# Loads of values, keys and queries planned one a step, and weight decoding kept out of the first and last round of an attention kernel

## The chip, the cores and the metric

One core of a Trainium2 chip runs the whole program. The metric is the device time of one execution in microseconds (us); lower is better. Kernels are compared by the median of several executions.

## The reference, cut to what matters

Four batches of attention over 12 heads, with a 12x12 mixing of the heads before and after the softmax, feed a two-layer network of 1792 tokens, 768 to 2048 to 768, with an ELU between the layers.

```python
scores = scale * q @ k.T                              # (4, 12, 448, 448), head_dim 64
scores = einsum('bhij,hg->bgij', scores, w_pre)
attn = exp(scores - max) / (sum + 1e-9)
attn = einsum('bhij,hg->bgij', attn, w_post)
x = (attn @ v) laid out as (1792, 768)
h = x @ moe_w_in;  g = where(h > 0, h, exp(min(h, 0)) - 1);  out = g @ moe_w_out
```

The two weight matrices arrive as 8-byte floats; the kernel makes 4-byte floats of them itself ("decoding").

## The kernel before, in words

**Attention.** `attention` (L127) works in 92 steps of one Python loop (L407, variable `j`), 23 for each batch; 23 steps are called a round here (`ROUND`, L376). A batch has four blocks of query rows, which take 5, 6, 6 and 6 steps, so that block 0 starts in step 0 of its round, block 1 in 5, block 2 in 11 and block 3 in 17. What one step does, in the order of the code: `norm` (L268) makes scaled copies `wz` of the post-mixing weights on GpSimd (POOL); `scores` (L249) mixes the raw scores of step j + 2 on TensorE (PE), from which VectorE (DVE) takes the maximum and ScalarE (ACT) the exponential; `send` (L234) starts the DMAs of raw scores computed in the step before; `av` (L299) multiplies by the values of an earlier block; `qk` (L207) computes four heads of raw scores of a later block and `keep_qk` copies them to SBUF; `post` (L280) mixes the heads of step j; then comes planned work (`work`, filled by `plan`, L371), most of it loads and splits of inputs.

**Raw scores.** The raw scores leave `qk` with a head in each tile, and `scores` wants the heads across partitions, so each head of each block is moved from SBUF to SBUF by a DMA on SyncE's queue (`raw<-st`, L242 and L245). A block's twelve heads are computed in three lots, at steps -10, -8, -6 (block 0), -4, -2, -1 (block 1), 1, 3, 5 (block 2) and 7, 9, 11 (block 3) of its round (`RAW_AT`, L377), and sent a step later each. `scores` of the block's first step is issued two steps ahead of that step: in steps -2, 3, 9 and 15 of the round. The last lot of block 2 is thus sent in step 6 and wanted in step 9. The first round differs: the last lot of its block 2 is computed in step 6 and sent in step 7.

**Inputs.** Values (`load_v`, six tiles a batch), keys (`load_k`, six) and queries (`load_q`, one tile a block) are loaded by DMAs that POOL issues (L203, L179, L191). Keys and queries are then split into a high and a low part on DVE and POOL (L185, L186, L197, L198), at fixed steps that the change leaves alone. `av` uses the values of a new batch from step 6 of its round on. A tile pool sets how early a load can go: there are eight buffers for values, four for keys, two for queries.

**Decoding.** `Weights.run` (L66) is a generator: each call of `step` advances it by one piece. A tile of weights takes four pieces: DVE operations L80, L85, L91 and L94, an ACT square L89 with the second, a load of 512 KB (L63) with the first and a store of 256 KB of the tile before (L103) with the second, both DMAs issued by POOL. There are 48 tiles, 24 of each matrix, in all 194 pieces and a last store. In the attention it is called at L436, in every even step from 8 on and in steps 21 and 61, 44 times. In the ELU stage it is called in `elu` (L609), and in the first matrix product after that eight pieces at a time (L684).

**Network.** From step 82 on the `Moe` class starts to load activations and decoded weights. Batches 0 and 1 go through `up` (L590) and `elu` (L601), then L692; batches 2 and 3 through seven products of half size on either side (L984 and L1046). Decoded tiles are read back from DRAM through SyncE's queue (`load_w`, L486), two blocks of hidden units ahead of their use (a block of 128 hidden units is 36 matmuls of `up`), and split into a high part on ACT (L513) and a low part on POOL or DVE (L514).

## Time and profile before

| | |
|---|---|
| three executions | 808.5, 812.62 and 818.0 us; median 812.62 |
| profiled execution | 811.77 us |
| its span, first to last instruction | 810.0 us |
| lies around the span | 1.77 us |
| mean granted clock of TensorE | 0.991 of full speed |
| PE busy in the span | 776.1 us (96%) |

A time of a row counts from the start of the span. The attention runs from about 18 to 356 us, and one round takes 84 us: the scores that are issued in step 9 of the second, third and fourth round start at 148.07, 231.78 and 315.43. The ELU stage of batches 0 and 1 runs to about 483, their second product to 600, and the seven products on either side fill the rest.

### The profile page before, as it was taken

What the parts mean: (1) busy time and instruction counts of PE and PEld (TensorE: products, weight loads), DVE (VectorE), ACT (ScalarE), POOL (GpSimd) and SP (SyncE); (2) the same over time, 40 slices, a digit from 0 to 9 for tenths busy, and PEclk for the clock granted to TensorE, in tenths of its full rate; (3) what the DMA queues carried; (4) which work ended last, traced back from release to release, by engine and by line L of the source; (5) the groups of instructions that cost most, each with busy time, mean ns of one, the idle gap of its engine ahead of it and who ended that gap; (6) DMA issues with size and microseconds to landing.
All of it is one profiled execution on the core that took longest, in us unless ns stands there. A gap on an engine that the chain in (4) does not pass through costs nothing.

```text
span 810.0 us, 25153 instructions
## 1 busy us (share of the span) xinstructions
PE 776.1 (96%) x10014; PEld 631.9 (78%) x10014; DVE 580.3 (72%) x1082; ACT 509.2 (63%) x1092; POOL 408.7 (50%) x529
## 2 busy tenths in 40 slices
PE   7787999899989999899999999999999999999998
PEld 3355676567656666678999999999999989899997
DVE  5685777686768676675988888776357777688962
ACT  3575878687867877785877783223157566665440
POOL 6574645464538353245787773275148877600000
PEclk9899999999999999999999999999999999999999
DMA  6568668756877685846998779987536866653331
GB/s 197 184 205 257 190 207 258 235 190 204 236 222 230 187 240 196 229 135 221 316 308 300 245 234 355 301 308 280 166 125 204 260 206 234 184 160 117 116 123 58
DMA packets 92845, 174.60 MB, mean 216 GB/s; under 512 B 21888, under 2 KB 59556, under 8 KB 92728
## 3 DMA queue, kind: packets, MB, share of 16 engines
q1 hardware_dynamic: 75288, 113.46, 43.7%
q0 software_dynamic: 16896, 58.61, 22.7%
q8 instruction: 79, 1.29, 0.6%
q10 hardware_dynamic: 544, 0.92, 0.3%
q14 instruction: 38, 0.31, 0.1%
HBM read 94.04 MB, written 39.35 MB: 165 GB/s over the span
## 4 chain that ended last, share of the span: by engine, by line
PE 79%; DMA 10%; POOL 3%; issue 3%; DVE 2%; ACT 2%; SPq 1%; POOLq 0%; ACTq 0%
PE h L597 15%; PE y L692 14%; PE y L1046 13%; PE mixed L287 9%; PE s L256 8%; PE xo L308 8%; PE qk L220 7%; PE h L984 6%; DMA raw<-st 4%; DMA sum<-mix 2%; DMA mix<-s 1%; POOL lo L841 1%; ACT p L263 1%; DMA wa<-in 1%; DVE nm L261 1%
## 5 line engine op out<-in xcount | busy, mean ns | idle before, releaser
L263 ACT ACTIVATE p<-s,nm 128x448 f32<-128x448 f32 x180 | 112.9, 634 | 54.2 <-DVE nm L261 53.6
L261 DVE TENSOR_REDUCE nm<-s 128x1 f32<-128x448 f32 x180 | 103.7, 617 | 56.9 <-PE s L256 56.5
L276 POOL TENSOR_SCALAR wz<-wb,rz 128x60 f32<-128x60 f32 x180 | 82.3, 469 | 107.8 <-DVE rz L272 48.0
L287 PEld LDWEIGHTS mixed<-wz,p 64*64 64x64 f32 x5040 | 85.9, 136 | 36.3 <-issue 25.8
L294 ACT COPY at<-mixed 128x480 f32<-128x480 f32 (+1 forms) x184 | 93.3, 566 | 32.1 <-PE mixed L287 30.5
L256 PE MATMUL s<-raw,wa 64*64 64x448 f32 x720 | 93.3, 553 | 16.8 <-DMA raw<-st 9.0
L287 PE MATMUL mixed<-wz,p 64*64 64x60 f32 x5040 | 100.1, 223 | 7.9 <-issue 5.6
L308 PEld LDWEIGHTS xo<-at,v 128*64 128x64 f32 x1536 | 75.8, 135 | 33.1 <-ACT st L230 24.0
L1046 PE MATMUL y<-part,hi 128*128 128x448 f32 x336 | 96.4, 367 | 0.0
L308 PE MATMUL xo<-at,v 128*64 128x120 f32 (+2 forms) x1536 | 86.8, 263 | 0.8 <-DMA v<-in 0.6
L513 ACT CAST hi<-lo 128x1024 fp32r<-128x1024 f32 (+1 forms) x49 | 48.0, 979 | 40.5 <-PE y L1046 34.6
L984 PE MATMUL h<-op,hi 128*128 128x448 f32 x264 | 72.2, 367 | 0.0
L597 PE MATMUL h<-xh,hi 128*128 128x448 f32 x192 | 70.7, 368 | 0.0
L597 PE MATMUL h<-xh,lo 128*128 128x448 f32 x192 | 70.1, 365 | 0.0
L597 PE MATMUL h<-xl,hi 128*128 128x448 f32 x192 | 70.1, 365 | 0.0
L692 PE MATMUL y<-gl,hi 128*128 128x448 f32 x192 | 69.8, 363 | 0.0
L692 PE MATMUL y<-gh,hi 128*128 128x448 f32 x192 | 69.8, 363 | 0.0
L692 PE MATMUL y<-gh,lo 128*128 128x448 f32 x192 | 69.7, 363 | 0.0
L514 DVE TENSOR_TENSOR lo<-lo,hi 128x1024 fp32r<-128x1024 f32 x30 | 37.9, 1263 | 42.2 <-ACT hi L513 40.1
L984 PE MATMUL h<-op,lo 128*128 128x448 f32 x240 | 67.4, 367 | 0.6 <-POOL lo L841 0.6
L1046 PEld LDWEIGHTS y<-part,hi 128*128 128x128 f32 x336 | 63.0, 188 | 6.3
L1046 PE MATMUL y<-part,lo 128*128 128x448 f32 x168 | 61.8, 368 | 0.0
(122 smaller groups left out, 1654.4 us busy)
## 6 DMA issues: line engine op xcount, KB each, us to landing
raw<-st SPq DMA_DIRECT2D x129, 210.0 KB
w<-in POOLq DMA_DIRECT2D x48, 512.0 KB, 6.0
lo<-s SPq DMA_DIRECT2D x58, 256.0 KB
s<-c POOLq DMA_DIRECT2D x48, 256.0 KB, 5.4
v<-in POOLq DMA_DIRECT2D x24, 256.0 KB, 6.6
lo<-half SPq DMA_DIRECT2D x16, 384.0 KB
lo<-sum SPq DMA_DIRECT2D x12, 512.0 KB
raw<-st SPq DMA_DIRECT2D x33, 175.0 KB
```

The lines of the kernel that those rows point to most:

```text
L220: nc.tensor.matmul(got[hh][:m, :S], q[part, hp, :m], k[part], start=i == 0, stop=i == 2)
L256: nc.tensor.matmul(ps[a][w * 64:(w + 1) * 64, :S], wa[half], raws[n % 2][half, ts[0] + w, :], start=True, stop=True)
L261: nc.vector.tensor_reduce(nm, ps[i][:, :S], op=ALU.max, axis=AX.X, negate=True)
L263: nc.scalar.activation(p, ps[i][:, :S], AF.Exp, bias=nm, scale=1.0, accum_out=z[:, i:i + 1])
L276: nc.gpsimd.tensor_scalar_mul(wz, wb, rz[:, i:i + 1])
L287: nc.tensor.matmul(mixed[w][half, i, c, :], p[part, j * 64:(j + 1) * 64], wz[part], start=True, stop=True)
L294: nc.scalar.copy(ats[n][:, :, ts[0]:ts[0] + len(ts), w, :], mixed[w][:, :len(ts)].rearrange("p t c n -> p c t n"))
L308: nc.tensor.matmul(ps[hh * 64:(hh + 1) * 64, w * m:(w + 1) * m].rearrange("p (t r) -> p t r", r=HR), vs[blocks[n][0], hp][:, c, hh * 64:(h ...
L597: self.nc.tensor.matmul(h, w[:, ks], x[:, k, :], start=n == 0, stop=n == 3 * NC - 1)
L692: nc.tensor.matmul(y[u], w[:, ks], g[f][:, u, :], start=f == 0 and n == 0, stop=f == NF - 1 and n == 2)
L984: nc.tensor.matmul(y, p[:, ks], x[:, z], start=q < 2 and k == 0 and n == 0, stop=k == KH - 1 and n == 2, skip_group_check=True)
L1046: nc.tensor.matmul(y, w[:, ks], g[:, x], start=begun is None and k == 0 and n == 0, stop=k == FH - 1 and n == 2, skip_group_check=True)
```

## The change

The loads of values, keys and queries get new steps, at most one load of them a step in each of the later rounds. Decoding starts in step 20 instead of 8, and ends with step 68, the last even one below `3 * ROUND`; the extra calls in steps 21 and 61 go. 25 pieces are decoded beside the attention instead of 44. The ELU stage takes 100 pieces instead of 88, and the product after it 69 or 70 instead of 62 or 63.

```diff
-LATE = 8
+LATE = 20
...
+    Q_AHEAD, V_AT = (7, 6, 6, 7), (19, 21, 24, 25, 26, 27)
...
-            plan(max(at[0] - 5, 1 - LOOK), lambda n=n: load_q(n, nc.gpsimd))
+            plan(max(at[0] - (Q_AHEAD[i] if b else 5), 1 - LOOK), lambda n=n: load_q(n, nc.gpsimd))
...
-                    plan(at[hp // 2] - 5, lambda b=b, hp=hp: load_k(b, hp, nc.gpsimd))
+                    plan(at[hp // 2] - 6 + hp % 2, lambda b=b, hp=hp: load_k(b, hp, nc.gpsimd))
...
-            if i == NB - 1 and b + 1 < B:
-                for w in range(2):
-                    plan(j + w, lambda b=b + 1, hp=2 * u + w: load_v(b, hp))
     for hp in range(NP):
         plan(hp + 2, lambda hp=hp: load_v(0, hp))
+        for b in range(1, B):
+            plan((b - 1) * ROUND + V_AT[hp], lambda b=b, hp=hp: load_v(b, hp))
...
-        if LATE <= j < N and (j % 2 == 0 or j % 40 == 21):
+        if LATE <= j < 3 * ROUND and j % 2 == 0:
             dec.step()
...
-        self.dec.step(2 + (u or f % 2))
+        self.dec.step(3 + (u and f % 4 == 0))
```

In steps of a round the loads move so: values of the next batch from 23, 24, 25, 26, 27, 28 (the last five are steps 1 to 5 of the round that uses them, the first its step 0) to 19, 21, 24, 25, 26, 27; keys of the next batch from 8, 8, 10, 10, 12, 12 to 7, 8, 9, 10, 11, 12; queries from 8, 14, 19, 25 to 6, 13, 18, 23. The first batch's values stay in steps 2 to 7.

On POOL's queue, around the end of the first round and the start of the second, the rows with a DMA or a split of queries stand as follows before (steps 24 to 28; `v` are values, `w` weights to decode, `s` the store of a decoded tile, `q` queries, `wz` the scaled weights that `post` waits for).

```order
L203 DMA v<-in 128x512
L276 TENSOR_SCALAR wz<-wb,rz 128x60 x2
L191 DMA q_2437<-in 128x720
L203 DMA v<-in 128x512
L276 TENSOR_SCALAR wz<-wb,rz 128x60 x2
L63 DMA w<-in 128x1024
L203 DMA v<-in 128x512
L276 TENSOR_SCALAR wz<-wb,rz 128x60 x2
L203 DMA v<-in 128x512
L276 TENSOR_SCALAR wz<-wb,rz 128x60 x2
L103 DMA s_1_74<-c 128x512
L198 TENSOR_TENSOR ql<-q_2437,qh 128x720
```

And now, in steps 22 to 27 (the two values loads of steps 19 and 21 stand ahead of it).

```order
L63 DMA w<-in 128x1024
L198 TENSOR_TENSOR ql<-q_1875,qh 128x720
L276 TENSOR_SCALAR wz<-wb,rz 128x60 x2
L191 DMA q_2268<-in 128x720
L276 TENSOR_SCALAR wz<-wb,rz 128x60 x2
L63 DMA w<-in 128x1024
L203 DMA v<-in 128x512
L276 TENSOR_SCALAR wz<-wb,rz 128x60 x2
L203 DMA v<-in 128x512
L276 TENSOR_SCALAR wz<-wb,rz 128x60 x2
L203 DMA v<-in 128x512
L276 TENSOR_SCALAR wz<-wb,rz 128x60 x2
```

The weights' load of step 26 and the store of step 28 have left this place, weights' loads stand in steps 22 and 24 instead, and the last value is issued a step earlier.

The second place is POOL's queue in steps 10 to 12 of the first round (`k` are keys of the second batch, `kl` their low part). Before:

```order
L63 DMA w<-in 128x1024
L179 DMA k_1230<-in 128x448
L179 DMA k_1232<-in 128x448
L276 TENSOR_SCALAR wz<-wb,rz 128x60 x2
L198 TENSOR_TENSOR ql<-q_1071,qh 128x720
L186 TENSOR_TENSOR kl<-k_1073,kh 128x448
L276 TENSOR_SCALAR wz<-wb,rz 128x60 x2
L63 DMA w<-in 128x1024
L186 TENSOR_TENSOR kl<-k_1075,kh 128x448
L179 DMA k_1404<-in 128x448
L179 DMA k_1406<-in 128x448
L276 TENSOR_SCALAR wz<-wb,rz 128x60 x2
```

Now:

```order
L179 DMA k_1228<-in 128x448
L276 TENSOR_SCALAR wz<-wb,rz 128x60 x2
L198 TENSOR_TENSOR ql<-q_910,qh 128x720
L186 TENSOR_TENSOR kl<-k_995,kh 128x448
L179 DMA k_1315<-in 128x448
L276 TENSOR_SCALAR wz<-wb,rz 128x60 x2
L186 TENSOR_TENSOR kl<-k_1073,kh 128x448
L179 DMA k_1397<-in 128x448
L276 TENSOR_SCALAR wz<-wb,rz 128x60 x2
```

One key's load now stands between the first low part and the `wz` behind it, one fewer behind the second low part, and the weights' loads are gone from here.

## Rows read from the trace of the kernel before

**Rows 1.** Busy time by stretch: length, PE, PEld, DVE, ACT, POOL, PEclk, DMA share, GB/s.
```profile
108.00:192.00 84.00, 80.58 (x1973) 55.52 (x1968) 61.57 (x149) 64.30 (x164) 45.33 (x78) 1.00 0.72 226
384.00:483.00 99.00, 99.00 (x490) 91.77 (x489) 84.47 (x134) 77.52 (x141) 76.10 (x79) 1.00 0.84 278
483.00:600.00 117.00, 117.00 (x584) 109.26 (x583) 78.49 (x106) 40.46 (x66) 46.70 (x64) 1.00 0.75 256
```
**Rows 2.** Timeline of PE, L256: start, duration, what, in brackets idle before and releaser.
```profile
63.43 0.98 PE L256 MATMUL s<-raw,wa 64*64 64x448 f32 x8 [2.75 <-DMA raw<-st]
...
125.63 0.98 PE L256 MATMUL s<-raw,wa 64*64 64x448 f32 x8 [0.27 <-DMA raw<-st]
...
148.07 0.98 PE L256 MATMUL s<-raw,wa 64*64 64x448 f32 x8 [2.35 <-DMA raw<-st]
...
231.78 1.77 PE L256 MATMUL s<-raw,wa 64*64 64x448 f32 x8 [2.09 <-DMA raw<-st]
...
315.43 0.98 PE L256 MATMUL s<-raw,wa 64*64 64x448 f32 x8 [1.50 <-DMA raw<-st]
```
**Rows 3.** Waits of the whole run: total, times, longest.
```profile
PE mixed L287 <- issue: 5.6, 7, 1.7
```
**Rows 4.** Timeline of PE, L287: the first and the last long one of these seven.
```profile
79.75 0.27 PE L287 MATMUL mixed<-wz,p 64*64 64x60 f32 x2 [1.48 <-issue]
...
342.14 0.51 PE L287 MATMUL mixed<-wz,p 64*64 64x60 f32 x19 [1.70 <-issue]
```
**Rows 5.** Busy time by stretch, columns of rows 1: the raw transfers of three rounds.
```profile
104.00:115.00 11.00, 11.00 (x240) 7.96 (x240) 7.25 (x19) 8.61 (x22) 3.27 (x7) 1.00 0.66 205
115.00:126.00 11.00, 10.73 (x296) 7.64 (x289) 8.51 (x22) 8.40 (x23) 6.95 (x13) 1.00 0.76 232
126.00:137.00 11.00, 11.00 (x274) 7.40 (x268) 8.42 (x21) 8.21 (x22) 4.58 (x10) 1.00 0.91 269
...
210.00:221.00 11.00, 11.00 (x274) 7.63 (x272) 8.40 (x21) 9.23 (x25) 5.34 (x10) 1.00 0.90 256
...
294.00:305.00 11.00, 10.47 (x262) 7.27 (x264) 8.29 (x21) 7.65 (x21) 4.12 (x9) 1.00 0.90 272
305.00:316.00 11.00, 9.50 (x260) 6.82 (x256) 6.45 (x17) 9.34 (x24) 5.31 (x10) 1.00 0.65 216
```
**Rows 6.** Timeline of POOL, 126 to 137 us: its DMA issues, start and duration.
```profile
126.26 0.58 POOL L63 DMA_DIRECT2D w<-in  x1
126.85 0.56 POOL L203 DMA_DIRECT2D v<-in  x1
...
130.47 0.59 POOL L203 DMA_DIRECT2D v<-in  x1
...
133.32 0.60 POOL L103 DMA_DIRECT2D s<-c  x1
```
**Rows 7.** DMA issues of the whole run: KB each, median us from issue to landing.
```profile
w<-in POOLq DMA_DIRECT2D x48, 512.0 KB, 6.0
...
s<-c POOLq DMA_DIRECT2D x48, 256.0 KB, 5.4
v<-in POOLq DMA_DIRECT2D x24, 256.0 KB, 6.6
...
q<-in POOLq DMA_DIRECT2D x14, 360.0 KB, 5.4
...
k<-in POOLq DMA_DIRECT2D x18, 224.0 KB, 5.9
```
**Rows 8.** Busy time by stretch, columns of rows 1: right after two of the waits.
```profile
63.00:68.00 5.00, 4.57 (x68) 3.13 (x72) 2.64 (x6) 2.29 (x6) 0.00 (x0) 0.66 0.77 274
...
232.00:237.00 5.00, 5.00 (x84) 2.72 (x80) 2.64 (x6) 2.51 (x7) 0.19 (x1) 0.70 0.63 190
```
**Rows 9.** Groups of instructions in 380 to 480 us: busy, mean ns of one, idle before.
```profile
L514 POOL TENSOR_TENSOR lo<-lo,hi 128x768 fp32r<-128x768 f32 (+1 forms) x14 | 26.5, 1892 | 0.0
...
L85 DVE SCALAR_TENSOR_TENSOR room<-w,room 128x512 int32<-128x512 int32 x20 | 13.9, 694 | 0.4
```

## The prediction

> **What bounds the kernel now.** I read the busy time by stretch first. In the ELU stage and the product behind it PE is busy all of 99.00 and 117.00 us [rows 1]; loads and decoding lie beside it, and what they cost there is nothing as long as it stays so. The attention is different: in a whole round of 84 us PE is busy 80.58, so 3.4 us of idle time are to be had, and DMA runs at a share of 0.72 on average [rows 1]. That is where this change can pay.
>
> Next, PE's timeline in the attention, for what ended each idle stretch. Two kinds stand out. The first is the wait of `scores` for the raw scores' transfers. It is there in five places [rows 2]: at the block 2 of all four rounds (2.75, 2.35, 2.09 and 1.50 us) and, short, at block 1 of the second round (0.27), 8.96 us together. The second kind falls into `post`, with no releaser that the profile shows ("issue"): 5.6 us in seven pieces [rows 3], from 79.75 to 342.14 [rows 4]. I take these for instructions of PE that arrive late, which is an inference: nothing in a row names it.
>
> Why always block 2? The busy time in stretches of 11 us shows it [rows 5]. The DMA share is 0.66, 0.76, 0.91 and it is 0.90 in the two later rounds in just the stretch (126 to 137, 210 to 221, 294 to 305) in which block 2's raw scores travel and behind which PE waits. POOL's timeline shows with what: between 126.26 and 133.32 it issues a load of weights, two of values and a store [rows 6], 512 + 256 + 256 + 256 KB [rows 7]. In the same stretch of 11 us 269 GB/s move, 2.96 MB [rows 5], so these four are 1.31 MB or 44% of it. One stretch earlier the share is 0.76, two earlier 0.66: there is room there.
>
> A wait costs more than its idle time. Behind the first and the fourth of the five the granted clock of the next 5 us is 0.66 and 0.70 on average [rows 8], which mixes the two levels; 5 x 0.34 = 1.7 us and 5 x 0.30 = 1.5 us of PE time went there.
>
> **The change part by part.** The sum is made against the profiled execution, 811.77 us, which lies 0.85 below the median of the runs, 812.62.
>
> Block 2, second round (2.35 us). The weights' load of step 26 and the store of step 28 leave the stretch, the values of steps 27 and 28 come a step earlier, one query is issued near its end. Of 1.31 MB some 0.5 stay, so about 0.8 MB of 2.96 go: 269 GB/s become about 197, less than the 205 at which no wait stands [rows 5]. I take -2.35; bounds 0 and -2.35.
>
> Block 2, fourth round (1.50). No decoding is left there and no query follows: the same 0.8 MB go, and the share 0.90 with them. -1.50; bounds 0 and -1.50.
>
> Block 2, third round (2.09, and 1.5 of clock). Here decoding stays: a load of weights moves from step 50 to 48, a store from 52 to 50, and a query (360 KB) comes in step 52. Of the traffic of the stretch 210 to 221 only about 0.25 MB goes, 256 GB/s become about 233, and that is the rate of the stretch with the 0.76, between no wait and a full one [rows 5]. I take half of both: -1.05 and -0.75; bounds 0 and -3.6.
>
> Block 2, first round (2.75). Its values stay in steps 2 to 7, and a query and a first key now come in steps 6 and 7, before the wait instead of after it: 360 + 224 KB [rows 7] at 263 to 274 GB/s are at most 2.2 us. Against that, the weights' loads of steps 8 and 10 go, but these were issued too late to hold it up. I take +0.5; bounds 0 and +2.2. Its clock loss stays.
>
> Block 1, second round (0.27). Here traffic is added: values in step 21, weights in 22 and 24, against a store in 21 and values in 23 before, some 0.75 MB more, over two stretches that now run at 205 and 232 GB/s [rows 5]. Spread over 22 us that is 34 GB/s, so they come to 239 and 266, just short of the 269 at which PE waits. At that rate 0.75 MB are 2.8 us. I take +1.0, nearer the stretch of 232; bounds -0.27 and +2.8. In the third and fourth rounds it is 0.1 to 0.36 MB: +0.3 each, bounds 0 and +1.3.
>
> The "issue" gaps (5.6). The one at 79.75 stands beside two weights' loads that go, the last at 342.14 beside decoding that goes too. If lateness comes with a full DMA, these have less of it now; if it comes with the place in the program, they only move. I take -2.0; bounds -5.6 and +3, as many again as half of those now seen.
>
> POOL's queue. A key's load (about 0.56 us on POOL, as in rows 6) now stands between the first `kl` and the `wz` behind it, so this `wz` is later by that in each of three rounds; PE asks for it one step on. POOL is busy 45.33 of 84 us [rows 1], and that is the cover: 0, and +1.7 if it is gone. The moved loads wait for no buffer: a value's buffer is free since step 23 or 25 of the round, and a key's since the split just ahead on the same queue. SP's queue has the same instructions in the same order.
>
> ELU stage. 12 more pieces at about 0.69 us [rows 9] are 8.3 us of DVE, which go from 84.47 to 92.8 of 99 [rows 1], 94%. PE fills up to six banks ahead of DVE, so a late DVE alone costs nothing at first. But the handing over gets tight. Counting pieces in the code, the read-back for hidden block 6 now follows the store that it needs by 2 pieces, for block 8 by 3, where it was 18 and 17. A hidden block is 36 matmuls, at 99.00 us for 490 [rows 1] 7.3 us, and a read-back is issued two blocks ahead of its use, 14.5 us. The store needs about 5.4 us to land, the read-back at most the 6.0 of a load of 512 KB [rows 7], the split 1.9 on POOL [rows 9] behind a shorter copy on ACT: some 14 us. It fits, narrowly. 0; bounds 0 and +8.3, if DVE sets the pace. In the product behind it 7 pieces are 4.8 us on a DVE that is busy 78.49 of 117: 0.
>
> Sum: -2.35 - 1.50 - 1.80 + 0.5 + 1.0 + 0.6 - 2.0 = -5.6, so 806.2 us.
>
> There is a rule that speaks against the first three terms. The rows show that DMA share alone does not tell whether raw scores are late: from 305 to 316, where PE waits 1.50, it is only 0.65 [rows 5]. The Trainium skill, "DMA: Bandwidth & Descriptors", section "Why a DMA increments its semaphore by 16 and not by 1", says that a DMA issued on SyncE uses the largest number of engines up to 16 that divides the slowest dimension on both sides; a raw score's transfer ends in 10 partitions, so by it on 10 of the 16. A mean share of 0.65 could then be those ten full, and a load over all 16 puts only 10/16 of its bytes in their way. By that rule the first three terms shrink to 10/16, from 5.65 to 3.5, and the sum would be 808.3. No row here splits the engines.
>
> **The rivals.** *All waits go* but that of the first round: 6.2 us of raw scores, 1.5 of clock and 5.6 of "issue", 13.3 us: 798.5. For it: the emptier first and last rounds, and every moved load goes toward a stretch of lower share. Against: the third round keeps its decoding.
>
> *The raw scores are slow by themselves.* Their own queue is the bound, and what shares the engines with it matters little: 305 to 316 has a share of 0.65 and yet the wait stands behind it. Then block 2 waits as before and only part of the gaps move: 811. Against: blocks 0, 1 and 3 send as many bytes with the same three steps to spare and wait next to nothing.
>
> *The waits move to block 1 and grow* (slower). Place: steps 3 of the second, third and fourth rounds, in which block 1 is wanted; the values of steps 19 and 21 and the weights of 20 to 24 lie ahead of it. Price: in the second round 1.0 MB at 269 GB/s, 3.7 us, in the others 0.5 MB, 1.9 each, and 1.7 of clock behind each: 12.6; with block 2 not relieved, 824.4. It decides as soon as the stretches of 0.66 and 0.76 go past 0.90. For it: block 1 already waits 0.27 in the second round. Against: what is added there is 34 GB/s.
>
> *Decoded weights come late in the ELU stage*: DVE at 94% falls behind, the narrow 14 of 14.5 us is overrun, and PE waits with DVE as the bound: 8.3 us on top of the forecast, 814.5. Against: the six banks, and in the trace of before no idle time of PE in 99 us.
>
> **How the numbers follow.** The forecast has 0.42, all waits gone 0.23, slow raw scores 0.16, late weights 0.10, waits at block 1 0.09. Around the forecast the unknown terms make 801 to 811. A measurement of this kernel tells about 1% from no change, 8.1 us: below 804.5 is faster, above 820.7 slower. Faster: all of 0.23 and three tenths of the forecast's 0.42, 0.36. Slower: the 0.09, and 0.01 for the tail of late weights. The rest, 0.54, is the same. The range reaches from 797, a little below all waits gone, to 817, which takes in late weights and leaves out block 1's case.
>
> **What would show it.** Right: the waits for raw scores at block 2 of the second and fourth rounds are gone from PE's timeline, that of the third is halved, the first's stays near 2.75; the share between steps 3 and 6 of a round falls from 0.90 toward 0.7 and rises between 20 and 2. PE stays at 99% and more in the ELU stage with DVE near 94%. Wrong: a wait of 2 us or more at block 1, waits at block 2 with a share below 0.8 around them, or PE idle between 384 and 600.

## The result and the profile after

The changed kernel takes 819.48 us (median of 22 executions, 811.53 to 825.23), the kernel before 813.92 in the same series (22, 806.68 to 822.37). The ratio is 1.0068, with a 95% interval of 1.0044 to 1.0092. A second series of 12 gave 1.0023 [0.9990, 1.0055] (below); weighted by executions the two make 1.0052 ("pooled" below), about 4 us slower. The forecast was 806.2 us, 5.6 under the execution that it started from, in a range of 797 to 817: its sign was wrong, and the time lies above the range.

The profiled execution of the changed kernel has a span of 817.3 us at a mean granted clock of 0.987, 7.3 us over that of before. First its busy time by stretch, columns of [rows 1]; each round starts a little later than before, so the stretches that answer to [rows 5] are moved by 2 to 6 us.

```profile
106.00:117.00 11.00, 10.95 (x221) 7.64 (x216) 5.96 (x16) 8.17 (x21) 3.77 (x8) 1.00 0.76 227
117.00:128.00 11.00, 10.71 (x298) 7.73 (x296) 8.12 (x22) 8.30 (x23) 6.57 (x12) 1.00 0.92 267
128.00:139.00 11.00, 7.58 (x132) 4.84 (x136) 4.56 (x10) 5.68 (x14) 2.62 (x6) 0.84 0.63 204
214.00:225.00 11.00, 10.06 (x243) 6.66 (x247) 7.79 (x20) 9.15 (x23) 4.63 (x10) 1.00 0.86 274
225.00:236.00 11.00, 8.84 (x200) 5.72 (x189) 5.01 (x12) 5.75 (x15) 3.97 (x8) 0.84 0.57 178
311.00:322.00 11.00, 10.48 (x279) 7.31 (x273) 6.73 (x19) 8.69 (x23) 4.35 (x8) 1.00 0.35 109
384.00:483.00 99.00, 96.94 (x499) 88.53 (x498) 86.32 (x138) 74.97 (x138) 76.48 (x82) 1.00 0.89 294
```

The share of 0.91 that stood at 126 to 137 [rows 5] now stands one stretch earlier (0.92), and behind it PE is busy only 7.58 of 11 us at a granted clock of 0.84, a mean over its two levels (1.2 and 2.4 GHz). The stage of the ELU, where PE had no idle time [rows 1], has 2.06 us of it.

PE's timeline of the changed kernel, the rows that answer to [rows 2] and [rows 4], with the new kinds of waits between them:

```profile
65.41 1.77 PE L256 MATMUL s<-raw,wa 64*64 64x448 f32 x8 [3.88 <-DMA raw<-st]
...
83.65 0.45 PE L220 MATMUL qk<-kl,qh 64*100 64x448 f32 x2 [0.95 <-POOL kl L186]
...
131.42 1.46 PE L256 MATMUL s<-raw,wa 64*64 64x448 f32 x8 [3.72 <-DMA raw<-st]
...
169.29 0.45 PE L220 MATMUL qk<-kl,qh 64*100 64x448 f32 x2 [1.35 <-POOL kl L186]
...
224.56 0.73 PE L287 MATMUL mixed<-wz,p 64*64 64x60 f32 x34 [0.94 <-issue]
...
230.72 0.34 PE L287 MATMUL mixed<-wz,p 64*64 64x60 f32 x2 [2.16 <-issue]
...
256.12 0.45 PE L220 MATMUL qk<-kl,qh 64*100 64x448 f32 x2 [1.91 <-POOL kl L186]
...
347.53 0.51 PE L287 MATMUL mixed<-wz,p 64*64 64x60 f32 x19 [1.08 <-issue]
...
400.29 0.47 PE L597 MATMUL h<-xh,lo 128*128 128x448 f32 x1 [0.27 <-POOL lo L514]
...
415.26 0.47 PE L597 MATMUL h<-xh,hi 128*128 128x448 f32 x1 [0.51 <-ACT hi L513]
...
417.21 0.47 PE L597 MATMUL h<-xh,lo 128*128 128x448 f32 x1 [1.28 <-POOL lo L514]
```

The waits at block 2 of rounds 2, 3 and 4 are gone. In their place stand a wait of 3.72 us at block 1 of the second round, one for the low part of a key in step 13 of each of the first three rounds, and three in the ELU stage. The gap called issue at 347.53 is that of 342.14 in [rows 4]: it stayed. The waits of the whole run, answering to [rows 3] (total, times, longest):

```profile
PE s L256 <- DMA raw<-st: 7.9, 3, 3.9
PE qk L220 <- POOL kl L186: 7.1, 6, 2.2
PE mixed L287 <- issue: 5.0, 4, 2.2
...
PE h L597 <- POOL lo L514: 1.6, 2, 1.3
```

SyncE's queue in the ELU stage (384 to 483 us) shows what is late there. Its read-backs of decoded tiles (L498) now wait until the store of the tile has landed (`s<-c`, L103); the same view of the kernel before has no such row.

```profile
SPq L498 <- DMA s<-c: 44.7, 16, 6.7
```

POOL's DMA issues ahead of that wait at block 1, the counterpart of [rows 6]: the first three pieces of decoding each load 512 KB, and they now lie in steps 20, 22 and 24, with a query and values beside them (other rows of POOL are left out).

```profile
107.21 0.58 POOL L63 DMA_DIRECT2D w<-in  x1
109.93 0.61 POOL L203 DMA_DIRECT2D v<-in  x1
114.26 0.58 POOL L63 DMA_DIRECT2D w<-in  x1
120.82 0.60 POOL L191 DMA_DIRECT2D q<-in  x1
122.25 0.58 POOL L63 DMA_DIRECT2D w<-in  x1
122.84 0.56 POOL L203 DMA_DIRECT2D v<-in  x1
```

### The profile page after: what moved, and what is told of

Its sections match the earlier page's. It is cut to its first block, busy times and chain, and to the rows that moved or that the text cites. A ratio compares the mean times of both kernels' runs of the same rounds, so it can differ in the third digit from the quotient of the medians.

```text
span 817.3 us, 25157 instructions
## 1 busy us (share of the span) xinstructions
PE 777.6 (95%) x10014; PEld 631.9 (77%) x10014; DVE 583.8 (71%) x1082; ACT 510.3 (62%) x1092; POOL 407.7 (50%) x529
## 4 chain that ended last, share of the span: by engine, by line
PE 76%; DMA 8%; issue 6%; POOL 5%; DVE 3%; ACT 1%; SPq 0%; POOLq 0%; ACTq 0%; DVEq 0%
PE y L692 14%; PE y L1046 13%; PE h L597 11%; PE mixed L287 8%; PE xo L308 8%; PE s L256 7%; PE h L984 7%; PE qk L220 6%; DMA raw<-st 2%; DMA sum<-mix 1%; POOL kl L186 1%; POOL lo L841 1%; POOL wz L276 1%; DMA q<-in 1%; DMA s<-c 1%
## 5 line engine op out<-in xcount | busy, mean ns | idle before, releaser
L276 POOL TENSOR_SCALAR wz<-wb,rz 128x60 f32<-128x60 f32 x180 | 80.2, 458 | 115.7 <-DVE rz L272 78.2
L287 PEld LDWEIGHTS mixed<-wz,p 64*64 64x64 f32 x5040 | 85.3, 136 | 34.4 <-issue 25.1
L256 PE MATMUL s<-raw,wa 64*64 64x448 f32 x720 | 94.4, 565 | 14.7 <-DMA raw<-st 7.9
L287 PE MATMUL mixed<-wz,p 64*64 64x60 f32 x5040 | 98.8, 223 | 7.0 <-issue 5.0
```

The costliest lines, as they stand in the source:

```text
L256: nc.tensor.matmul(ps[a][w * 64:(w + 1) * 64, :S], wa[half], raws[n % 2][half, ts[0] + w, :], start=True, stop=True)
L276: nc.gpsimd.tensor_scalar_mul(wz, wb, rz[:, i:i + 1])
L287: nc.tensor.matmul(mixed[w][half, i, c, :], p[part, j * 64:(j + 1) * 64], wz[part], start=True, stop=True)
```

## The experiments

Eighteen kernels were run. One profile holds one execution, and executions of one kernel spread by some 15 us, so two things are compared throughout: the ratio to the kernel before, and the length of a few steps, which each profile shows. A step's length here is the time between the first L256 rows of two successive `scores` on PE's timeline; "8+9" is the length of the steps whose `scores` start there (block 2's wait and the low clock behind it), "2+3" the same for block 1, "12+13" the steps with the waits for split keys. us:

| kernel | 12+13, rounds 1-3 | 8+9, round 1 | 8+9, rounds 2-4 | 2+3, round 2 | 2+3, rounds 3, 4 | ratio [95%] |
|---|---|---|---|---|---|---|
| before | 23.77 | 10.92 | 27.92 | 7.06 | 13.56 | 1 |
| changed | 25.25 | 12.75 | 19.98 | 12.06 | 13.57 | 1.0068 [1.0044, 1.0092] |
| e9: changed, again | 25.08 | 11.93 | 20.96 | 8.76 | 15.94 | 1.0023 [0.9990, 1.0055] |
| e1: new loads only | 25.30 | 13.07 | 25.16 | 6.79 | 18.41 | 1.0010 [0.9976, 1.0044] |
| e2: new decoding only | 23.69 | 13.34 | 19.97 | 9.14 | 13.60 | 0.9986 [0.9955, 1.0016] |
| e3: keys old | 23.30 | 7.40 | 19.98 | 13.23 | 16.49 | 0.9999 [0.9962, 1.0036] |
| e7: fifth key old | 23.71 | 13.19 | 20.26 | 10.57 | 14.53 | 1.0006 [0.9967, 1.0045] |
| e8: first keys old | 25.11 | 12.72 | 19.97 | 8.80 | 14.86 | 0.9994 [0.9959, 1.0029] |
| e4: first pieces early | 25.66 | 11.95 | 20.59 | 7.46 | 15.47 | 0.9983 [0.9951, 1.0015] |
| e17: queries old | 25.41 | 13.45 | 20.07 | 6.86 | 14.65 | 1.0003 [0.9972, 1.0033] |
| e5: keys old, pieces early | 24.59 | 9.20 | 19.97 | 6.79 | 14.29 | 0.9954 [0.9912, 0.9996] |
| e6: and old pace in the ELU | 23.92 | 10.77 | 20.78 | 7.99 | 16.18 | 0.9948 [0.9916, 0.9981] |
| e12: before, new keys | 25.26 | 10.90 | 30.11 | 6.83 | 13.56 | 1.0048 [1.0015, 1.0081] |
| e13: before, fifth key moved | 25.22 | 8.96 | 27.47 | 7.29 | 14.03 | 1.0010 [0.9976, 1.0044] |
| e11: before, decoding moved | 25.21 | 7.25 | 21.80 | 6.87 | 14.71 | 0.9949 [0.9912, 0.9986] |
| e10: e11, new queries | 23.92 | 14.72 | 19.98 | 8.41 | 15.25 | 1.0013 [0.9978, 1.0048] |
| e14: e11, all new loads but the fifth key | 24.00 | 14.44 | 24.88 | 7.69 | 15.20 | 0.9966 [0.9936, 0.9997] |
| e15: e11, new keys | 25.72 | 14.42 | 20.22 | 6.80 | 13.57 | 0.9996 [0.9954, 1.0038] |
| e16: e11, new values | 23.71 | 6.70 | 20.04 | 6.78 | 13.58 | 0.9929 [0.9897, 0.9960] |
| e18: e16, again | 24.52 | 8.47 | 20.19 | 6.87 | 13.57 | 0.9959 [0.9921, 0.9998] |

A single ratio is uncertain by some 0.35%, a difference of two by some 0.5%; where several pairs differ in the same edit, their mean is given.

**The two halves apart (e1, e2).** e1 is the changed kernel with the old decoding, e2 the kernel before with the new one.

```diff
-LATE = 20
+LATE = 8
...
-        if LATE <= j < 3 * ROUND and j % 2 == 0:
+        if LATE <= j < N and (j % 2 == 0 or j % 40 == 21):
...
-        self.dec.step(3 + (u and f % 4 == 0))
+        self.dec.step(2 + (u or f % 2))
```

This is e1 against the changed kernel; e2 has the same three lines the other way, against the kernel before.

> The kernel before with the new plan of value, key and query loads alone; decoding is called as before. Theory 1 (the new decoding plan costs: its first weight loads fall on block 1 of the second round, and the ELU stage waits for weights): the wait at step 26 is under 1 us, the ELU stage has no idle time of PE, and the time is 0.4 to 1.0% below the changed kernel's, at or under the kernel before (ratio 0.993 to 1.002). Theory 2 (the key's load between the two key splits on the GpSimd queue costs): PE waits 0.9 to 1.9 us for the low part of a key in step 13 of the first three rounds as in the changed kernel, and the ratio to the kernel before stays at 1.003 or above.

> The kernel before with the new decoding plan alone (steps 20 to 68, 100 pieces in the ELU stage); loads as before. Theory 1: PE waits 1.5 us or more at step 26 and about 2 us in the ELU stage, block 2 waits as before in the second and third round and less in the first and fourth; ratio to the kernel before 1.002 to 1.008. Theory 2: no wait for the low part of a key over 0.8 us, and the ratio is 0.995 to 1.001, as the emptier rounds pay.

Steps 8 and 9 of rounds 2 to 4 fall from 27.92 to 19.97 us with the decoding alone and only to 25.16 with the loads alone. In e2 block 2 of these rounds does not wait at all; in e1 it waits 1.33 us in the second round and 1.63 in the third. So it is the decoding that takes these waits off. But e2 gains next to nothing in time. Neither theory holds whole: e1 has theory 1's ratio and its quiet ELU stage, but in rounds 2 and 3 also theory 2's waits for split keys (1.28 and 1.61 us); e2 has theory 1's wait at step 26, but theory 2's ratio, and 0.26 us of waiting in the ELU stage instead of about 2. PE's timeline of e2, its two waits of more than 2 us for raw scores:

```profile
66.18 1.77 PE L256 MATMUL s<-raw,wa 64*64 64x448 f32 x8 [4.11 <-DMA raw<-st]
...
131.38 0.98 PE L256 MATMUL s<-raw,wa 64*64 64x448 f32 x8 [2.27 <-DMA raw<-st]
```

The second is at block 1, 0.27 in the kernel before [rows 2]; there the new decoding makes it without any load moved. In e1 block 1 waits in another place, the last round:

```profile
298.04 1.44 PE L256 MATMUL s<-raw,wa 64*64 64x448 f32 x8 [2.40 <-DMA raw<-st]
```

**The keys (e3, e12, e7, e8, e13).** e3 puts all keys back in the changed kernel, e12 moves them alone in the kernel before. e7 puts back one load, the fifth key from step 11 to 12 (the sixth is at 12 in both); e13 moves just that load in the kernel before; e8 puts back the first and third.

e3, against the changed kernel (e12 has it the other way, against the kernel before):

```diff
-                    plan(at[hp // 2] - 6 + hp % 2, lambda b=b, hp=hp: load_k(b, hp, nc.gpsimd))
+                    plan(at[hp // 2] - 5, lambda b=b, hp=hp: load_k(b, hp, nc.gpsimd))
```

The same line in e7, e8 (both against the changed kernel) and e13 (against the kernel before):

```diff
+                    plan(at[hp // 2] - (6 if hp < 4 else 5) + (hp % 2 if hp < 4 else 0), lambda b=b, hp=hp: load_k(b, hp, nc.gpsimd))
...
+                    plan(at[hp // 2] - (5 if hp < 4 else 6) + (0 if hp < 4 else hp % 2), lambda b=b, hp=hp: load_k(b, hp, nc.gpsimd))
...
+                    plan(at[hp // 2] - 5 - (hp == 4), lambda b=b, hp=hp: load_k(b, hp, nc.gpsimd))
```

> The changed kernel with the key loads back at their steps of before (two in steps 8, 10 and 12), so that both follow the second split. Theory 2: the waits for the low part of a key in step 13 (0.95, 1.35 and 1.91 us) fall under 0.5 us each, and the time is 2 to 4 us below the changed kernel (ratio to the kernel before 1.002 to 1.004). Theory 1: it stays within 1.5 us of the changed kernel (ratio 1.005 to 1.009), with 3 us or more of waiting at step 26.

> The changed kernel with only the last two of the six key loads of a block at their old step (both at step 12), the first four as in the change (7, 8, 9, 10). Theory A (the cost of the new key plan is the load that POOL issues between the last two splits, in the same step): the waits of PE for split keys at step 13, 0.45 to 1.91 us in the changed kernel, fall to under 0.8 us, and the ratio comes down from 1.0068 to about 1.001 to 1.003. Theory B (the cost is the key moved to step 7 and the spread of the first four, which meet the raw scores and the weights): the ratio stays at 1.005 to 1.008.

> The reverse: the first four key loads at their old steps (8, 8, 10, 10), the last two as in the change (11, 12). Theory A (the load between the last two splits): the waits for split keys stay at 0.5 to 1.9 us a round, and the ratio stays at 1.005 to 1.008. Theory B (the key at step 7): the ratio comes down to 1.000 to 1.002, and the first round's steps 8 and 9 are together under 10 us (12.8 in the changed kernel).

> The kernel before, with only the key loads at the new steps (7, 8, 9, 10, 11, 12). Theory A (the new key steps cost by themselves, through the split on POOL): ratio 1.004 to 1.008, with waits for split keys of 0.5 to 1.9 us at step 13. Theory B (they cost only beside the decoding that now lies in the same steps of rounds 2 and 3 with fewer gaps): ratio 0.998 to 1.002, and the waits for split keys sum to no more than in the kernel before (the new waits under 0.5 us each).

> The kernel before, with one load of six moved one step: the fifth key of a batch at step 11 instead of 12, so that POOL issues it between two splits. Theory A (this load is most of the key plan's cost): the second low part of step 12 starts 2.8 to 2.9 us after the first (2.13 in the kernel before), PE waits for split keys in step 13 by 0.5 us or more a round, and the ratio is 1.002 to 1.005. Rival (0.7 us a round on POOL is paid by what PE waits for anyway): the same rows on POOL, but steps 12 and 13 grow by under 0.6 us a round and the ratio is 0.998 to 1.002.

In e12 PE's timeline shows the wait for split keys in step 13 of rounds 1 to 3, without any new decoding, and the ratio is theory A's:

```profile
83.23 0.45 PE L220 MATMUL qk<-kl,qh 64*100 64x448 f32 x2 [1.53 <-POOL kl L186]
...
168.79 0.45 PE L220 MATMUL qk<-kl,qh 64*100 64x448 f32 x2 [1.26 <-POOL kl L186]
...
254.82 0.45 PE L220 MATMUL qk<-kl,qh 64*100 64x448 f32 x2 [1.60 <-POOL kl L186]
```

What the one load does is plain on POOL's timeline of the kernel before and of e13, steps 11 and 12 of the second round.

```profile
161.17 1.13 POOL L186 TENSOR_TENSOR kl<-k,kh 128x448 fp32r<-128x448 f32 x1
162.29 1.04 POOL L276 TENSOR_SCALAR wz<-wb,rz 128x60 f32<-128x60 f32 x2
163.30 1.15 POOL L186 TENSOR_TENSOR kl<-k,kh 128x448 fp32r<-128x448 f32 x1
164.39 1.16 POOL L179 DMA_DIRECT2D k<-in  x2
```

e13:

```profile
161.75 1.13 POOL L186 TENSOR_TENSOR kl<-k,kh 128x448 fp32r<-128x448 f32 x1
163.18 0.62 POOL L179 DMA_DIRECT2D k<-in  x1 [0.30 <-DVE nm L261]
163.84 0.84 POOL L276 TENSOR_SCALAR wz<-wb,rz 128x60 f32<-128x60 f32 x2
164.65 1.12 POOL L186 TENSOR_TENSOR kl<-k,kh 128x448 fp32r<-128x448 f32 x1
166.07 0.60 POOL L179 DMA_DIRECT2D k<-in  x1 [0.30 <-POOL kl L186]
```

Before, both loads stand behind the second split; now one stands between the two, 0.62 us after 0.30 us of waiting. (The releaser named there is an instruction of DVE; by the code the load waits for the buffer that the split just ahead gives back, and for the next load the row names the second split.) The second split starts 2.90 us after the first instead of 2.13. Steps 12 and 13 of three rounds grow by 25.22 - 23.77 = 1.45 us, and to 25.1 or more in every kernel with the fifth key at 11; with it at 12 they take 23.3 to 24.6, save e11 (25.21, with three gaps called issue in them). In e7 the wait for split keys is nearly gone from the whole run (7.1 us in the changed kernel, 4.2 of them in step 13):

```profile
PE qk L220 <- POOL kl L186: 1.0, 4, 0.4
```

In the length of these steps that is 1.5 us or 0.18%. The whole key plan costs more: the four pairs that differ in it alone (changed, pooled, against e3; e12 against before; e15 against e11; e4 against e5) give 0.53, 0.48, 0.47 and 0.29%, on average 0.44%. e3's ratio (0.9999) lies under theory 2's range, though 4.34 us of waiting at step 26 stay, as theory 1 has it. Of theory A in e7's expectation the rows hold, and its ratio is a little under. That the one load is most of the price does not follow. e13 goes to the rival: its rows on POOL are those that both expect, but steps 12 and 13 grow by 0.48 us a round, PE does not wait for split keys in step 13 of the first round, and the ratio is 1.0010. e8 keeps the load between the splits and the length of these steps (25.11) and is no slower than e7; its ratio is theory B's, but steps 8 and 9 of its first round take 12.72 us and not under 10.

One more sum can be made. Three pairs differ in the fifth key alone (changed, pooled, against e7; e13 against before; e8 against e3): 0.46, 0.10 and -0.05%, on average 0.17%, about the 1.5 us of the rows. Three differ in the other moved keys alone (changed, pooled, against e8; e7 against e3; e14 against e6): 0.58, 0.07 and 0.18%, on average 0.28%. No single pair resolves either, and where the second part arises stays open.

**The first pieces (e4), and keys besides (e5, e6).** In e4 the three pieces that load 512 KB each are taken out of steps 20, 22 and 24. e5 has the keys old as well; e6 moreover decodes to the end of the attention and keeps the old pace in the ELU stage.

The line of e4 and e5, against the changed kernel (the key's line in e5 is that of e3), then the two of e6:

```diff
-        if LATE <= j < 3 * ROUND and j % 2 == 0:
+        if j in (12, 14, 16) or 26 <= j < 3 * ROUND and j % 2 == 0:
```

```diff
-        if LATE <= j < 3 * ROUND and j % 2 == 0:
+        if j in (12, 14, 16) or 26 <= j < N and j % 2 == 0:
...
-        self.dec.step(3 + (u and f % 4 == 0))
+        self.dec.step(2 + (u or f % 2))
```

> The changed kernel with the first three decoding pieces in steps 12, 14 and 16 instead of 20, 22 and 24; all else equal, so that no load of weights is issued between steps 17 and 30. Theory 1: the wait of 3.72 us at step 26 falls under 1 us, the clock behind it stays at its higher level, and the time is 4 to 5 us below the changed kernel (ratio to the kernel before 1.000 to 1.003). If the values in steps 19 and 21 are what makes block 1 late, 2 us or more of the wait stay and the time moves by less than 2 us.

> The changed kernel with both single mendings at once: the keys at their old steps (two a step, five before use), and the first three pieces of decoding at steps 12, 14 and 16 rather than 20, 22 and 24. Theory A (the two costs are separate): the keys cost 0.7% and the late first pieces 0.85%, as the two single runs gave, and they add, so the ratio to the kernel before comes to 0.991 to 0.994 (806 to 809 us). The second round's block 1 waits less than 1 us for its raw scores, no wait for split keys is over 0.8 us, and rounds 2 to 4 show no wait in block 2. Theory B (both mendings take off the same wait, since weights, keys and queries stand in the same queue in steps 12 to 28): the ratio is that of the single mendings, 0.997 to 1.000. Theory C (values at steps 19 and 21 now meet block 1): the waits of block 1 in rounds 3 and 4 sum to over 4 us and the ratio is over 1.000.

> As the run with both mendings, and besides decoding goes on to the end of the attention at even steps and the stage of the ELU issues pieces at the pace of the kernel before. Theory A (the lead of the weights was cut too far: the split weights of the ELU stage come late): the two waits of that stage for the split weights (1 to 2 us in the changed kernel) are under 0.3 us, and the ratio is 0.1 to 0.25% under that of the run with both mendings. Rival: the last round's block 2 waits again for raw scores (1.5 us in the kernel before), because the weight loads stand beside it, and the ratio is the same or up to 0.2% higher.

The pairs with late and early pieces (changed, pooled, against e4; e3 against e5; e2 against e11, which differs in its last pieces and in the ELU's pace too) give 0.69, 0.45 and 0.37%, on average 0.50%. In e4 the wait at step 26 falls to 0.68 us, as theory 1 has it, and the ratio to 0.9983, under its range. e5 and e6 beat the kernel before by 0.5%; e5's ratio lies between its theories A and B, and neither is decided. In e6 the rival's wait at the last round's block 2 did not come. The ELU stage has no idle time of PE in e6:

```profile
384.00:483.00 99.00, 99.00 (x490) 91.73 (x489) 84.39 (x135) 79.83 (x145) 76.53 (x81) 1.00 0.85 280
```

This separates cleanly over all profiles: with the old pace PE has no wait over 0.2 us for split weights of that stage, with the new one these waits make 0.26 to 2.06 us. The pace and the end of decoding beside the attention were always changed together, so no run tells them apart. SyncE's wait for stores there falls with them, from 51.1 us in e5 to 11.7 in e6. The time of e6 against e5 does not resolve it.

**The changed kernel again (e9).**

> The changed kernel once more, beside the three others of this call and the same runs of the kernel before. Theory A (the loss of 0.68% is the change's own): the ratio is 1.004 to 1.010, and the second profile shows the same waits as the first: split keys at step 13 of rounds 1 to 3 (0.3 us or more each), raw scores of block 1 in the second round (over 1 us), the split weights of the ELU (over 0.5 us). Rival (the first measurement was off, since each of four partial mendings came to 0.998 to 1.001): the ratio is under 1.003. What of the first profile's waits is not in the second is chance of one execution; the gaps called issue at 224.56 and 230.72 us are expected to be at other places.

1.0023 is the rival's by the letter, but its interval, 0.9990 to 1.0055, reaches into theory A's range, so it decides nothing by itself. The kinds of waits came back, with smaller sizes: split keys in step 13 of three rounds (0.95, 0.47, 0.66 us), and on PE's timeline

```profile
129.22 0.98 PE L256 MATMUL s<-raw,wa 64*64 64x448 f32 x8 [1.90 <-DMA raw<-st]
...
230.97 0.98 PE L256 MATMUL s<-raw,wa 64*64 64x448 f32 x8 [1.01 <-DMA raw<-st]
...
294.33 0.98 PE L256 MATMUL s<-raw,wa 64*64 64x448 f32 x8 [1.45 <-DMA raw<-st]
...
409.08 0.47 PE L597 MATMUL h<-xh,lo 128*128 128x448 f32 x1 [0.24 <-POOL lo L514]
```

The two long gaps called issue at 224.56 and 230.72 did not come back in this profile. Block 2 of the first round waits 3.91 us, much as in the first profile (3.88).

**The loads one by one beside the better decoding (e11, e10, e16, e15, e14), and the queries put back in the changed kernel (e17).**

e11, against the kernel before:

```diff
-        if LATE <= j < N and (j % 2 == 0 or j % 40 == 21):
+        if j in (12, 14, 16) or 26 <= j < N and j % 2 == 0:
```

e10, e16 and e15 are e11 with the change's lines for the queries, the values and the keys alone; e14 is e6 with the key's line of e7. e17, against the changed kernel:

```diff
-            plan(max(at[0] - (Q_AHEAD[i] if b else 5), 1 - LOOK), lambda n=n: load_q(n, nc.gpsimd))
+            plan(max(at[0] - 5, 1 - LOOK), lambda n=n: load_q(n, nc.gpsimd))
```

> The kernel before, with only its decoding beside the attention moved: pieces at steps 12, 14, 16 and at even steps from 26 to the end, and all loads of values, keys and queries as before. Theory A (the decoding plan alone carries the gain, the load plan none): the ratio is 0.993 to 0.997, as the runs with old keys, and rounds 2 to 4 show no wait over 1 us for raw scores in block 2. Rival (the loads of queries and values matter as well): the ratio is 0.998 or more, and block 2 of round 2 or 3 waits again, by 1 to 2.4 us.

> As the run with both mendings and the lead (old key steps, first pieces at 12, 14, 16, then every even step to the end), with the values at their old steps too, so that of the new load plan only the queries are left. Theory A (values at steps 19 and 21 hold up block 1's raw scores in rounds 3 and 4): the waits there, 0.69, 0.83 and 1.91 us in that run, go, and the ratio falls from 0.9948 to 0.990 to 0.993. Rival (the values planned one a step are what took load off the stretch of steps 21 to 28): waits of over 2 us come back at block 2 or block 1, and the ratio is 0.997 or more.

> The kernel with the better decoding alone (0.9949), with the new steps of the values added and nothing else. Theory A (values cost nothing, and gain nothing once the decoding is out of the way): 0.993 to 0.997. Rival (the loads at steps 19 and 21 make block 1 wait): waits for raw scores in step 3 of rounds 2 to 4 sum to over 3 us, and the ratio is 0.998 or more. The wait for raw scores in block 2 of the first round, which no part of this touches before 68 us, is expected anywhere from 0.6 to 6 us, as kernels that are the same up to there have shown.

> The kernel with the better decoding alone (0.9949), with the new key steps added and nothing else. Theory A (the keys cost by themselves, 0.3 to 0.5%, whatever stands beside them): 0.998 to 1.000, waits for split keys at step 13 of 0.5 to 1.6 us in rounds 1 to 3. Rival (they cost only where the traffic is dense): 0.994 to 0.997.

> First pieces of decoding at 12, 14, 16, then every even step from 26 to the end, with the whole new load plan but for the fifth key, which is at step 12 as before. Theory A (that load is the only harm in the load plan): the ratio is 0.993 to 0.997, as with all loads old (0.9949). Rival (queries, or keys beside decoding, cost by themselves): 0.999 or more.

> The changed kernel with only the queries at their old steps. Theory A (the query issued in step 0 stands beside the last lot of block 1's raw scores): steps 2 and 3 of rounds 3 and 4 take 13.5 to 14.0 us together (13.57 and 15.94 in the two profiles of the changed kernel, 15.5 on average over the kernels with new queries), and the ratio is 1.000 to 1.003. Rival (the values at steps 19 and 21 do it): over 15 us, and the ratio stays at 1.004 or more. In the second round block 1 still waits over 1 us, since the first pieces of decoding stay late, and the waits for split keys stay.

e11 is as theory A has it in time; but one wait of 1.55 us for raw scores stays at block 2, in the last round, where it decodes on, and theory A had none over 1 us. e16 is theory A's, a hair under its range. e15 falls to theory A (the keys cost by themselves), e14 lies at the upper edge of theory A, and e10 goes to the rival, though not by the waits at block 2 that the rival names, save in the first round.

My reading after the first runs, that values at steps 19 and 21 hold up block 1, fell: with new values and old queries (e16, e18) its steps in rounds 3 and 4 take 13.58 and 13.57 us, as before; with new queries and old values (e10) 15.25. Over all profiles the mean is 15.47 with new queries (11) and 13.87 with old (9). A round's last query, 360 KB, is now issued in step 0 of the next, together with the last lot of block 1's raw scores, instead of step 2. e17's ratio is theory A's; its steps 2 and 3 of rounds 3 and 4 take 14.65 us, between theory A and the rival, with a gap called issue of 0.70 us in them and no wait for raw scores. The only such wait left in e17 is that of the first round's block 2:

```profile
PE mixed L287 <- issue: 7.4, 7, 2.1
PE s L256 <- DMA raw<-st: 4.7, 1, 4.7
```

There block 1 does not wait in the second round either (6.86), against what I expected; steps 2 and 3 of that round, by pieces and queries (means, profiles):

| | queries old | queries new |
|---|---|---|
| first pieces in 20, 22, 24 | 8.0 (2) | 10.7 (5) |
| first pieces in 12, 14, 16 | 6.8 (4) | 7.7 (5) |

Most of the wait comes with the two together: late pieces alone add 1.2 us (2.3 in e2, none in e17), new queries alone 0.8, both 3.9. In time the queries cost 0.49 (changed, pooled, against e17), 0.64 (e10 against e11) and 0.04% (e6 against e16 and e18, pooled), 0.39% on average. No cost of the values shows: e16 and e18, pooled, are 0.05% under e11, and e6 is 0.65% under e10.

**The best one again (e18).**

> The better decoding with the new steps of the values, once more. Theory A (it beats both kernels): the ratio is 0.990 to 0.996 again, steps 8 and 9 of rounds 2 to 4 take about 20 us and steps 2 and 3 of them about 20.4. Rival (the first measurement was a good draw of a kernel worth no more than the decoding alone): 0.996 to 1.000.

0.9929 and 0.9959: on average 0.9944, 4.6 us faster than the kernel before. It is the kernel before with decoding at 12, 14, 16 and from 26 on in even steps, and with the values planned one a step, and it beats both. The second series alone lies at the border of theory A and the rival. That the values add anything to the better decoding alone (e11, 0.9949) is not shown.

## Why the prediction was wrong, point by point

**Block 2, rounds 2 to 4: right, undersized.** Forecast -5.65 in three terms; steps 8 and 9 of these rounds fell by 7.9 us in the first profile and 7.0 in the second. The half kept in the third round wasn't there in the first profile; in the second 1.01 us of waiting are. That the waits go when the decoding goes (e2) speaks against the rival of raw scores slow by themselves. My working from the Trainium skill, "DMA: Bandwidth & Descriptors", section "Why a DMA increments its semaphore by 16 and not by 1", by which these terms would have shrunk to 3.5, is not borne out. That section of the Trainium skill says how many engines a transfer uses, and no run here shows that number; what it means for a load beside the transfer was my own step.

**Block 1, second round: the step that failed most.** Forecast +1.0, at most 2.8; steps 2 and 3 grew by 5.0 us (3.45 of wait, the rest in the step behind it, at the lower clock) and by 1.7 in the second profile. Over the five profiles with late first pieces and new queries they take 10.7 us, 3.6 more than before and beyond the bound. The rates were forecast well (239 and 266 GB/s; 227 and 267 came). What failed is the threshold read from them, that PE waits at 269 and not short of it. The profile after has the counterexample on both sides: 267 GB/s and a wait of 3.72 us, and in block 2's stretch of the third round (214 to 225) 274 GB/s and no wait. Place and price in this round were those of the rival in which the waits move to block 1 (3.7 us and 1.7 of clock), which had 0.09, and its condition came in the second of its two stretches: the share went past 0.90, to 0.92. A share does not settle it by itself either: PE waited 1.50 us behind one of 0.65 [rows 5]. So a mean over 11 us did not tell here whether a transfer is late. The runs point to what is issued close to its last lot. I had spread 0.75 MB over 22 us, of which a query (120.82) and a load of weights (122.25) stand beside that lot. Even that is not the whole: with the same late pieces and old queries e2 waits 2.27 us and e17 not at all.

**Block 1, rounds 3 and 4.** Forecast +0.6; 0.0 and +2.4 in the two profiles, about +1.6 by the means above: the queries, which I priced only in bytes.

**POOL's queue: 0, and it cost 1.5 and 1.3 us.** I followed the key's load to the `wz` behind it and stopped; behind that `wz` stands the second `kl`, which PE asks for at once. And the load does wait for a buffer, 0.30 us for the split just ahead, where I wrote that it waits for none. The bound of 1.7, "if it is gone", came near, but it priced the `wz`; that it fits the delay of the second `kl` is luck.

**ELU stage: 0, and it cost 2.1 and 0.5 us.** The narrow 14 of 14.5 us was overrun, as in the rival of late weights, but not for its reason: DVE did not set the pace, it is busy 86.32 of 99 us, not 92.8. PE's waits end with the splits on POOL and ACT, and these two had been idle themselves: ahead of the wait of 1.28 us at 417.21 ACT stood idle 3.87 us before its high part and POOL 3.60 before its low part. What came late was the tile, since its read-back waits for the store to land, 44.7 us in 16 times, up to 6.7, where the sum had 5.4 for a store.

**"Issue" gaps: -2.0.** 5.6 us before, 5.0 and 3.1 in the two profiles after, and 1.7 to 7.4 over all twenty, with 6.4 and 7.4 in e16 and e17, whose waits for raw scores are among the smallest. The prediction had two readings, and the twenty profiles tell them apart for its two gaps. The last one, at 342.14, lies in step 85; a gap called issue of 0.26 to 1.70 us stands there in 18 of the 20 profiles, and in the changed kernel, with no decoding left in that round, it is still 1.08 and 1.11 us. That one comes with the place in the program, and not with the decoding beside it, which e11 (0.26) and e18 (1.70) both have. So, it seems, do those in steps 73 and 58, in 12 and 11 of the 20 profiles. The first one, at 79.75 in step 12, is in three of the four profiles with the old decoding and in none of the others, so it seems to have gone with the weights' loads. What makes these gaps stays open.

**Block 2, first round.** +0.5 forecast, +1.8 and +1.0 came. No run resolves this term (next section but one).

The rows account for the sign and not for the whole size. The first profile adds up: -7.9 + 1.8 + 5.0 + 1.5 in these steps, 1.9 behind the last `scores`, 4.7 in the other steps between the first and the last (most of it in steps 51 to 53, with the issue gaps at 224.56 and 230.72, which the second profile does not have) and 0.3 ahead of the first are 7.3, up to rounding. In the second profile the same places make -7.0 + 1.0 + 4.1 + 1.3, 0.7, -1.4 and 0.9, -0.3 us, although the median of its series lies 1.1 us over that of the kernel before. By the ratios of the single runs the parts come to 0.44 (keys) + 0.50 (late first pieces) + 0.39 (queries) - 0.51% (the better decoding, e11), 0.82% together, against 0.52 measured: the three costs outweigh the gain, but none is known to better than some 0.3%. And the kernel before's profiled execution was a low draw: 811.77 beside a median of 813.92 of the later series, 2.15 of the 13.3 us by which the forecast missed.

## What to carry to other kernels

Before planning loads "one a step", see that no step puts a load beside the last lot of a transfer that is due next, or between two instructions of a queue that another engine waits for; follow a moved issue past every instruction behind it, not only the next one. When decoding is kept out of a busy stretch, see where its first pieces land, since these are all loads, and how close a read-back then follows its store. And read a wait from several executions before giving it a price.

## What the runs showed of the hardware that was not expected

The same transfer's wait in the same program varies from one execution to the next: block 1's in the second round is 3.72 and 1.90 us in the two profiles of the changed kernel. e5, e6 and e10 have the same instructions up to step 19 of the first round, and their PE timelines, each from its own profile, show at block 2 of that round:

```profile
63.91 0.98 PE L256 MATMUL s<-raw,wa 64*64 64x448 f32 x8 [2.55 <-DMA raw<-st]
```

```profile
63.50 1.09 PE L256 MATMUL s<-raw,wa 64*64 64x448 f32 x8 [2.63 <-DMA raw<-st]
```

```profile
68.45 1.77 PE L256 MATMUL s<-raw,wa 64*64 64x448 f32 x8 [6.30 <-DMA raw<-st]
```

The five waits of [rows 2] were such draws, and the prediction took each at its face value.

A DMA issue on POOL that needs, by the code, a buffer released by the instruction just ahead on the same queue leaves 0.30 us idle before its 0.62 (e13). In the kernel before, where the load behind the split needs another buffer, long free, and only the load after that needs the split's, the two take 1.16 together with no idle time shown.
